# Reordering the second batch's attention and moving one cast in a fused attention and gated-MLP kernel

## The chip, the cores and the metric

The kernel runs on one core of one Trainium2 chip. The metric is the device time of one execution in microseconds. Three executions of the kernel before took 326.76, 326.96 and 328.4 us; the median is 326.96.

A core has five instruction streams that run side by side and wait for one another through semaphores: TensorE (PE, matrix products, with a separate row PEld for its weight loads), VectorE (DVE), ScalarE (ACT), GpSimd (POOL) and SyncE (SP, which here only issues DMA transfers). Each stream executes its own instructions in the order in which they were written. Sixteen DMA engines move data. Matrix products are accumulated in PSUM, a small memory that the other engines read from; everything else on the core lives in SBUF.

## The reference

```python
def _attn_ref(q, k, v, g_norm):            # 8 batches, 8 heads, 576 positions, 64 columns
    kv = np.einsum('bhsd,bhse->bhde', k, v)
    out = np.einsum('bhsd,bhde->bhse', q, kv)
    rms = np.sqrt(np.mean(out * out, axis=-1, keepdims=True) + 1e-06)
    return (out / rms * g_norm)

def _moe_ref(x, w_gate, w_val, w_out, rms_g):   # 4608 tokens, 512 columns, 1536 inner columns
    rms = np.sqrt(np.mean(x * x, axis=-1, keepdims=True) + 1e-06)
    xn = x / rms * rms_g
    g = xn @ w_gate
    return (g * (1 / (1 + np.exp(-g))) * (xn @ w_val)) @ w_out
```

The attention has no softmax: each head forms a 64x64 matrix `kv` and multiplies q by it. Its output is normalised per head, laid out as 4608 rows of 512, and goes through a gated MLP that normalises each row again.

## The kernel before

**Tiling.** A batch has 576 positions: four chunks of 128 (`NC = 4`) and a remainder of 64. The heads are handled in pairs, four pairs (`NS = 4`). The MLP handles 512 positions at a time: group g is batch g without its remainder, and a last group, the ninth, takes the eight remainders, which are collected in `xr`. So the MLP of group g needs the attention of batch g, and while PE works on group g the attention of batch g + 1 is fitted between its matmuls.

**The MLP of a group** (L630 to L704). For each of 12 blocks of inner columns there is a gate slot (four matmuls into a PSUM tile of the pool `mm1`, then silu on ScalarE, L643) and a value slot (four matmuls, L634, then the product with the silu on VectorE, L652). Then 16 slots of three L669 matmuls multiply by `w_out`; the result is copied out of PSUM (L685) and stored by a DMA that SP issues. The first group (batch 0) is done differently, since its inputs come late: its 512 positions go in two halves of 256, so the gate and value matmuls are half as wide (12 pairs per half), and its second product runs over all four output tiles at once (`slots_b_by_j`, L728). Two of these four output tiles are in the pool `o2` and two in `mm1`, which has three buffers; the third was left over in these slots.

**Slots and order.** The second half of group 0 is 12 slots of one gate and value pair each (slots 0 to 11), then 16 slots of three L669 matmuls (12 to 27); group 1 begins with slot 28, which is `starts[1]`. A `Placer` holds a list of operations for each slot. `P.at(engine, cost, function, slot)` puts an operation into a given slot; `P.put` searches the first slot from a given one that has room for it on its engine, by costs and room that are written in tables (L21 to L28), and `P.psum` does it for PE work that needs one of the three `att` buffers in PSUM. `emit` (L746) then walks through the slots: first the other engines' operations of a slot, then the slot's own MLP matmuls, then its attention work on PE. This is the order in which every engine executes.

**The attention of batch 1** (`place_second`, L577, called with s = 9). All its places are written out by hand, as offsets from s. The steps:

- `qT_heads` (L304): transposes of q on PE, copied out by VectorE and ScalarE (L320).
- `kv_mm` (L260): 40 matmuls of 64 columns that form `kv` of all heads in one `att` buffer, and `kv_half` (L290), two copies of it on VectorE to SBUF (`kvs`).
- `oT_mm` (L363): the attention output transposed, one PSUM tile for each head pair (and one for the remainder); `sqT_` (L374) squares it on ScalarE into `sqT`.
- `o_mm` (L328): the attention output itself, one PSUM tile for each chunk; `outa_` (L359) copies it to SBUF as bf16 on VectorE, which frees its `att` buffer.
- `stat_mm` (L399): 20 small matmuls of `sqT` with the selection matrix `sel` (L407), which sum the squares per head, plain and weighted by the squared gain. With `guard=True` one more matmul (L402, in fp32, two passes in the profile) first writes `D * eps` into the plain sums, so that they are never zero.
- `lead_chain` (L428): from these sums the factor `al` for each row and head: a reciprocal, a product, a sum, one more operation on VectorE, a square root on ScalarE (its table is loaded ahead by `preload_act_table`, L608, and silu's after it, L441), and a reciprocal.
- `xna_` (L479): output times factor, one instruction for each chunk, on VectorE.
- `xT_mm` (L502) and `xT_out` (L515): transposes on PE for the MLP, two chunks and two head pairs at a time, copied out with the gain by ScalarE (pairs `P0`) and VectorE (pairs `P1`).

In `place_second` oT and o of a part come in turn, o is copied, and the guard is PE's.

**The attention of batches 2 to 7** (`place_attention`, L553) is placed by searching. It takes its squares from o, multiplies them by the squared gain on POOL (L414), and computes the factor on VectorE. q is transposed by DMA on SP (L324, L326) once it has been cast to bf16; k and v are loaded and cast by DMAs that POOL issues (L185: 512 KB and a remainder of 64 KB each); x is transposed by DMA on SP (L540). The cast of q comes from `place_casts` (L542): for batch 2 on ScalarE at three given slots, the first being `starts[1] - 9`, and it returns the slot from which q's transposes count as done; for later batches on POOL. Batch 3's k and v loads and its casts of q are put on POOL's list from group 1's slots 14 and 18 on.

## Time and profile before

| what | value |
|---|---|
| executions | 326.76, 326.96, 328.4 us |
| the profiled execution: time, and span from its first to its last instruction | 326.35 us, 324.6 us |
| mean granted clock of TensorE | 0.999 |
| PE busy, 37 to 62 us | 24.72 of 25.00 us |
| PE busy, 62 to 94 us | 32.00 of 32.00 us |
| DMA traffic, 37 to 62 us and 62 to 94 us | 203 and 158 GB/s |
| SP's transposes of batch 2's q, issued | 57.19 and 58.72 us |
| SP's transposes of batch 2's x, issued | 86.13 and 88.08 us |

The page gives, for one execution, the busy time of each engine and the chain of work that ended last, followed back from the end. A line of a timeline gives the start in us, the duration, the engine, the line of the kernel, the operation, output <- input with shapes, how many instructions were merged into the line, and in brackets the idle time before and what ended it. PE's matmuls overlap: a matmul of 512 columns is shown with 0.38 us, and the next starts 0.216 us after it. ScalarE and VectorE instructions overlap by about 0.1 us in the same manner. DMA rows give the size of a transfer and the time from its issue to its landing.

Group 0's second half ends at 44.81 us, its second product at 59.68 us; group 1 ends at about 93.8 us.

### The profile page before, as it was taken

To read this page: it belongs to the slowest core of one execution; us is meant where nothing else is said; L and a number is where in the kernel's file an instruction comes from. 1 tells how busy PE (TensorE), PEld (TensorE's weight loads), DVE (VectorE), ACT (ScalarE), POOL (GpSimd) and SP (SyncE) were. 2 spreads that over 40 slices of the span, in tenths; PEclk is the share of its full clock that TensorE was granted. 3 is DMA by queue.
4 is the path that set the end of the run, shared out by engine and by line. 5 is a ranking of instruction groups with operands and counts; after the bars stand their busy time and mean duration, and the time that the engine had idled before them with its cause. 6 is when DMAs were issued, how large, how long until landed. Compare 5 with 4: busy or idle time off the path is not lost.

```text
span 324.6 us, 5420 instructions
## 1 busy us (share of the span) xinstructions
PE 316.2 (97%) x2060; PEld 162.2 (50%) x2060; DVE 177.0 (55%) x392; ACT 144.5 (45%) x269; POOL 89.4 (28%) x109
## 2 busy tenths in 40 slices
PE   7889999999999999999999999999999999999995
PEld 2478865554454445444544445444544444444443
DVE  3458457679938671858186818681778133203411
ACT  1375546686658323832284227422742233223320
POOL 8753330039106700670058005800420000000000
PEclk9999999999999999999999999999999999999999
DMA  8999999965994995499558956796100800020013
GB/s 194 228 200 200 191 220 221 203 161 72 163 210 124 127 162 142 140 118 149 147 158 101 139 149 178 87 138 165 35 1 0 172 32 0 29 102 0 0 34 97
DMA packets 78741, 40.49 MB, mean 125 GB/s; under 512 B 42744, under 2 KB 74236, under 8 KB 78716
## 3 DMA queue, kind: packets, MB, share of 16 engines
q0 software_dynamic: 30928, 14.16, 34.4%
q1 hardware_dynamic: 46048, 25.08, 32.6%
q10 hardware_dynamic: 1740, 0.92, 1.0%
q8 instruction: 16, 0.26, 0.3%
q14 instruction: 9, 0.07, 0.1%
HBM read 37.78 MB, written 9.44 MB: 145 GB/s over the span
## 4 chain that ended last, share of the span: by engine, by line
PE 95%; DMA 3%; DVE 1%; issue 0%; POOL 0%; ACT 0%; DVEq 0%; POOLq 0%
PE mm L634 57%; PE o L669 26%; DMA vc<-in_v_dram 3%; PE att L331 2%; PE att L268 2%; PE mm L669 2%; PE o L698 1%; PE att L509 1%; PE o L368 0%; PE mm L279 0%; PE att L368 0%; PE mm L662 0%; PE att L309 0%; PE mm L232 0%; PE att L340 0%
## 5 line engine op out<-in xcount | busy, mean ns | idle before, releaser
L652 DVE TENSOR_TENSOR h<-silu,mm 128x512 bf16<-128x512 bf16 (+1 forms) x120 | 75.7, 632 | 84.5 <-PE mm L634 78.7
L643 ACT ACTIVATE silu<-mm 128x512 bf16<-128x512 f32 (+1 forms) x120 | 66.3, 555 | 83.0 <-PE mm L634 73.7
L634 PE MATMUL mm<-x,wv 128*128 128x512 bf16 (+1 forms) x432 | 99.8, 355 | 0.0
L634 PE MATMUL mm<-x,wg 128*128 128x512 bf16 (+1 forms) x420 | 98.7, 358 | 0.0
L669 PE MATMUL o<-wo,h 128*128 128x512 bf16 x396 | 89.9, 379 | 0.0
L414 POOL TENSOR_TENSOR sq<-sq,g 128x512 bf16<-128x512 bf16 x30 | 34.7, 1156 | 130.9 <-ACT sq L357 130.9
L634 PEld LDWEIGHTS <-wv 128*128 128x128 bf16 x480 | 46.2, 98 | 44.0
L634 PEld LDWEIGHTS <-wg 128*128 128x128 bf16 x468 | 44.6, 98 | 42.4
L669 PEld LDWEIGHTS <-h 128*128 128x128 bf16 x420 | 40.3, 98 | 46.9
L685 ACT COPY osb<-o 128x512 f32<-128x512 f32 x33 | 19.2, 587 | 69.5 <-PE o L669 69.5
L419 DVE TENSOR_REDUCE st<-sq 128x8 f32<-128x512 bf16 x60 | 38.9, 678 | 1.2 <-ACT sq L357 0.8
L292 DVE CAST kvs<-att 64x256 bf16<-64x256 f32 x14 | 5.9, 422 | 29.9 <-PE att L268 29.7
L483 DVE TENSOR_TENSOR xna<-outa,al 128x512 bf16<-128x512 bf16 x35 | 21.8, 684 | 0.0
L357 ACT ACTIVATE sq<-att 128x512 bf16<-128x512 f32 x30 | 17.9, 596 | 2.2 <-PE att L331 2.2
L361 ACT CAST outa<-att 128x512 bf16<-128x512 f32 x30 | 17.7, 589 | 0.0
L331 PEld LDWEIGHTS <-qTs 128*128 128x128 bf16 x140 | 10.3, 98 | 6.6
L331 PE MATMUL att<-kvs,qTs 128*128 128x128 bf16 x140 | 12.7, 219 | 0.0
L634 PE MATMUL mm<-xr,wg 128*128 128x512 bf16 x48 | 12.3, 379 | 0.0
L634 PE MATMUL mm<-xr,wv 128*128 128x512 bf16 x48 | 12.3, 379 | 0.0
L203 POOL CAST main_q<-stg 128x1024 bf16<-128x1024 f32 (+1 forms) x12 | 11.4, 997 | 0.1
L232 PE MATMUL mm<-idle 128*128 128x512 bf16 x27 | 8.4, 471 | 2.1 <-DVE idle L161 2.1
L786 ACT ACTIVATE wv<-wv,gain 128x384 bf16<-128x384 bf16 x16 | 9.1, 609 | 0.0
(130 smaller groups left out, 172.3 us busy)
## 6 DMA issues: line engine op xcount, KB each, us to landing
out_dram<-osb SPq DMA_DIRECT2D x32, 256.0 KB, 2.4
stg<-in_q_dram SPq DMA_DIRECT2D x6, 1024.0 KB, 6.5
vc<-in_v_dram POOLq DMA_DIRECT2D x7, 512.0 KB, 8.4
kc<-in_k_dram POOLq DMA_DIRECT2D x7, 512.0 KB, 6.1
wg<-in_moe_w_gate_dram POOLq DMA_DIRECT2D x4, 384.0 KB, 15.8
wv<-in_moe_w_val_dram POOLq DMA_DIRECT2D x4, 384.0 KB, 16.9
wo<-in_moe_w_out_dram POOLq DMA_DIRECT2D x4, 384.0 KB, 13.8
stg<-in_k_dram SPq DMA_DIRECT2D x2, 512.0 KB, 6.7
```

The source lines that it names most:

```text
L203: return copy(out=mains[b, t][:, cs[0] : cs[1], h0:h1, :], in_=staged[b, t].rearrange("p h (c d) -> p c h d", c=NC)[:, cs[0] : cs[1], h0:h ...
L331: nc.tensor.matmul(o[:, 2 * j : 2 * j + 2, :], lhsT=self.qTj[:, j, c, :], rhs=self.kv[:, j, :, :], start=j == 0, stop=j == NS - 1, skip_gr ...
L357: nc.scalar.activation(out=self.sq[c][:, 0], in_=self.o[c], func=ACT.Square)
L361: (eng.tensor_copy if eng else nc.scalar.copy)(out=self.outa[c], in_=self.o[c])
L414: eng.tensor_tensor(out=self.sq[c][:, 1], in0=self.sq[c][:, 0], in1=g2, op=OP.mult)
L419: nc.vector.reduce_sum(out=self.st[:, which, c, :], in_=self.sq[c][:, which], axis=AX.X)
L483: return eng.tensor_tensor(out=self.xna[:, c], in0=src, in1=self.al[:, c, :].to_broadcast([128, H, D]), op=OP.mult)
L634: nc.tensor.matmul(ps[:, : c1 - c0], lhsT=w[n][:, s, jj * 128 : (jj + 1) * 128], rhs=x_of(g, s, c0, c1), start=s == 0, stop=s == NS - 1)
L643: nc.scalar.activation(out=sis[g, j][:, c0:c1], in_=ps, func=ACT.Silu)
L652: nc.vector.tensor_tensor(out=hs[g, j][:, c0:c1], in0=sis[g, j][:, c0:c1], in1=v_ps, op=OP.mult)
L669: nc.tensor.matmul(ps, lhsT=hs[g, j][:, t * 128 : (t + 1) * 128], rhs=wo[j // OB][:, j % OB, :], start=j == 0, stop=j == NF - 1)
L685: (eng.copy if eng is nc.scalar else eng.tensor_copy)(out=o, in_=ps)
```

## The change

For batch 1, `kv_mm` moves from slot s + 2 to s, and its copies from s + 3 to s + 1. All five oT steps come first, then the statistics (at s + 6 in place of s + 8), then the five o steps. o is no longer copied to SBUF: `xna_` reads it from PSUM, which holds each o tile until its product; the third of them uses the free buffer of `mm1`. The guard is added by VectorE in `lead_chain`, with one `tensor_scalar`, and not by a matmul. The products and the final transposes come three slots sooner, with the two transposes of a pair one slot apart. The floor for the next batch's PE work goes from slot s + 20 to s + 18. For batch 2, the three operations that cast q on ScalarE move from slots 19 to 21 to slots 24 to 26, and the slot from which q's transposes count as done from 30 to 32. The tables and all other batches' code are the same; what is placed by searching may come out at other slots. Behind the edit the line numbers are three lower (L634 becomes L631).

```diff
-        def stat_mm(self, c0, c1, guard=False):
+        def stat_mm(self, c0, c1):
             self.st = st = att_p.tile([128, 2, NC + 1, H], FP32, name="att")
-            if guard:
-                nc.tensor.matmul(
-                    st[:, 0, c0:c1, :], lhsT=ones, rhs=epsr[:, : (c1 - c0) * H], start=True, stop=True, skip_group_check=True,
-                )
...
-                        start=not guard and c == c0 and j == 0, stop=c == c1 - 1 and j == NS - 1,
+                        start=c == c0 and j == 0, stop=c == c1 - 1 and j == NS - 1,
...
-        def lead_chain(self, c0, c1):
+        def lead_chain(self, c0, c1, guard=False):
...
             u = self.st[:, 0, cs]
+            if guard:
+                u = self.u[:, cs]
+                V.tensor_scalar(out=u, in0=self.st[:, 0, cs], scalar1=D * eps, scalar2=None, op0=OP.add)
             V.reciprocal(out=r, in_=u)
...
-            return [op, ("DMA", at + 11)]
+            return [op, ("DMA", at + 8)]
...
-        P.at("PE", 1.14, lambda: a.kv_mm(range(NS)), s + 2)
-        dve(3, 0.43, lambda: a.kv_half(0))
-        dve(3, 0.43, lambda: a.kv_half(1))
+        P.at("PE", 1.14, lambda: a.kv_mm(range(NS)), s)
+        dve(1, 0.43, lambda: a.kv_half(0))
+        dve(1, 0.43, lambda: a.kv_half(1))
 
         parts = [((j,), 0, NC) for j in range(NS)] + [(ALL, NC, NC + 1)]
-        oT = lambda n: pe((3, 4, 4, 5, 6)[n], 0.25, ("oT", n), lambda: a.oT_mm(*parts[n]))
-        o = lambda n: P.at("PE", 0.24, lambda: a.o_mm(n), s + (3, 4, 5, 5, 6)[n])
-        for f, n in ((oT, 0), (o, 0), (oT, 1), (o, 1), (oT, 2), (o, 2), (oT, 3), (o, 3), (oT, 4), (o, 4)):
-            f(n)
         for n in range(NC + 1):
-            act((4, 5, 5, 6, 7)[n], 0.62, lambda n=n: a.sqT_(ps["oT", n], *parts[n]))
-            dve((4, 5, 6, 6, 7)[n], 0.69, lambda n=n: a.outa_(n, V))
-        P.at("PE", 0.64, lambda: a.stat_mm(0, NC + 1, True), s + 8)
-        act(8, 1.28, lambda: A.preload_act_table(ACT.Sqrt))
-        dve(9, 2.0, lambda: a.lead_chain(0, NC + 1))
+            pe((2, 2, 3, 4, 5)[n], 0.25, ("oT", n), lambda n=n: a.oT_mm(*parts[n]))
+            act((3, 4, 4, 5, 6)[n], 0.62, lambda n=n: a.sqT_(ps["oT", n], *parts[n]))
+        act(6, 1.28, lambda: A.preload_act_table(ACT.Sqrt))
+        P.at("PE", 0.64, lambda: a.stat_mm(0, NC + 1), s + 6)
+        for n in range(NC + 1):
+            P.at("PE", 0.24, lambda n=n: a.o_mm(n, mm1_p if n == 2 else None), s + (7, 7, 8, 9, 10)[n])
+        dve(7, 2.2, lambda: a.lead_chain(0, NC + 1, True))
         for c in range(NC + 1):
-            dve(10 + c, 0.68, lambda c=c: a.xna_(c, V))
-        for at, cs in ((15, (0, 1)), (17, (2, 3))):
-            for js, eng in ((P0, "ACT"), (P1, "DVE")):
-                P.at("PE", 0.24, lambda js=js, cs=cs: a.xT_mm(js, cs), s + at)
+            dve(9 + c, 0.68, lambda c=c: a.xna_(c, V, a.o[c]))
+        for at, cs in ((12, (0, 1)), (14, (2, 3))):
+            for n, (js, eng) in enumerate(((P0, "ACT"), (P1, "DVE"))):
+                P.at("PE", 0.24, lambda js=js, cs=cs: a.xT_mm(js, cs), s + at + n)
                 for j in js:
-                    P.at(eng, 0.4, lambda j=j, cs=cs, e=engs[eng]: a.xT_out(j, cs, e), s + at + 1)
-        P.at("PE", 0.15, lambda: a.xT_mm(ALL, (NC,)), s + 19)
-        dve(20, 0.62, lambda: [a.xT_out(j, (NC,), V) for j in ALL])
-        P.floor = s + 20
+                    P.at(eng, 0.4, lambda j=j, cs=cs, e=engs[eng]: a.xT_out(j, cs, e), s + at + n + 1)
+        P.at("PE", 0.15, lambda: a.xT_mm(ALL, (NC,)), s + 16)
+        dve(17, 0.62, lambda: [a.xT_out(j, (NC,), V) for j in ALL])
+        P.floor = s + 18
...
-            casts = place_casts(P, 2, starts[1] - 9)
+            casts = place_casts(P, 2, starts[1] - 4)
```

## The prediction

> **What bounds the kernel now.** I read the page first, the busy rows and the chain.

> ```profile
> span 324.6 us, 5420 instructions
> PE 316.2 (97%) x2060; PEld 162.2 (50%) x2060; DVE 177.0 (55%) x392; ACT 144.5 (45%) x269; POOL 89.4 (28%) x109
> PE   7889999999999999999999999999999999999995
> PE 95%; DMA 3%; DVE 1%; issue 0%; POOL 0%; ACT 0%; DVEq 0%; POOLq 0%
> ```

> TensorE works nearly all the time and is 95% of the chain that ended last. So a change is worth only the gaps it takes out of PE or puts in. By stretch, PE is busy 24.72 of 25 us from 37 to 62 and 32.00 of 32 from 62 to 94. The edit lies in the first stretch; nothing there can give more than its gaps and the PE work it drops. Second, PE in order of time around the second batch's attention:

> ```profile
> 44.00 0.88 PE L268 MATMUL att<-vc,kc 128*64 128x64 bf16 x40
> 45.26 0.38 PE L669 MATMUL mm<-wo,h 128*128 128x512 bf16 x1
> 45.91 0.39 PE L368 MATMUL att<-qTs,kvs 128*128 128x512 bf16 x1 [0.28 <-DVE kvs L292]
> 51.45 0.41 PE L402 MATMUL att<-epsr,ones 1*128 1x40 f32 x2
> 51.80 0.65 PE L407 MATMUL att<-sel,sqT 128*128 128x4 bf16 x20
> 59.68 1.03 PE L634 MATMUL mm<-x,wg 128*128 128x512 bf16 x4
> ```

> A wait of 0.28 for the kv copies, the guard (0.34 in the chain), and batch 1's first gate at 59.68. Third, where the next edge is: POOL's list and the landings of batch 3's k and v, and what PE does with them (columns of the loads: size, us from issue to landing).

> ```profile
> 75.51 0.94 POOL L192 DMA_DIRECT2D kc<-in_k_dram  x1
> 76.46 1.16 POOL L414 TENSOR_TENSOR sq<-sq,g 128x512 bf16<-128x512 bf16 x1
> 77.56 2.02 POOL L203 CAST main_q<-stg 128x1024 bf16<-128x1024 f32 x2
> 79.53 0.60 POOL L210 CAST remq<-rstg 64x512 bf16<-64x512 f32 x1
> 80.09 0.75 POOL L188 DMA_DIRECT2D kc<-in_k_dram  x1
> 81.70 0.70 POOL L188 DMA_DIRECT2D vc<-in_v_dram  x1
> ```

> ```profile
> kc<-in_k_dram POOLq DMA_DIRECT2D x1, 512.0 KB, 6.0
> vc<-in_v_dram POOLq DMA_DIRECT2D x1, 512.0 KB, 8.4
> kc<-in_k_dram POOLq DMA_DIRECT2D x1, 64.0 KB, 4.4
> vc<-in_v_dram POOLq DMA_DIRECT2D x1, 64.0 KB, 9.4
> x<-xna SPq DMA_TRANSPOSE x2, 5.5
> ```

> ```profile
> 92.35 0.88 PE L268 MATMUL att<-vc,kc 128*64 128x64 bf16 x40
> 93.16 0.82 PE L669 MATMUL o<-wo,h 128*128 128x512 bf16 x3
> 93.82 1.03 PE L634 MATMUL mm<-x,wg 128*128 128x512 bf16 x4
> ```

> The last v load lands at 81.70 + 9.4 = 91.1, kv needs it at 92.35. The second transpose of batch 2's x is issued at 88.08 and taken alone lands 5.3 later, at 93.4; the gate at 93.82 needs it. Only 1.2 and 0.4 us are spare there.

> **The change, part by part.**

> *kv sooner.* PE runs 12 groups of half width from 38.66 to 43.9, 0.437 each. kv moves ahead of the last four, to 42.16. Its copies (0.86 on VectorE) hide behind four groups, 1.75: the 0.28 goes. Without that cover it would be back. The second 64 KB of k was issued at 26.97 and landed 13.8 later, 40.8, so 1.4 us are spare.

> *Guard.* Two matmuls, 0.34, leave PE. VectorE gets one addition on 128x40, 0.21 (L455), 0.25 with its gap.

> *oT first, o in PSUM.* PE's operations stay the same. From the end of the half groups, 44.81, PE needs 48 L669 at 0.216 = 10.37, five oT 1.08, statistics 0.59, five o 1.10, four xT groups 0.90. The statistics follow twelve L669 and five oT: 44.81 + 2.59 + 1.08 = 48.48, done 49.1. From the reciprocal to the first product took 1.84 (52.49 to 54.33); with the addition 2.09, so products run from 51.4, one each 0.60. A product from PSUM takes 682 ns (L350, 128x512), from SBUF 684 (L483): no price, and five copies of 690 leave VectorE, which is not on the path. Held buffers: the fifth o needs the first product (52.1) and comes at 44.81 + 24 L669 + 1.08 + 0.59 + 0.88 = 52.5, 0.4 spare, the smallest margin; the first xT comes at 54.1 and needs the second product at 52.7. The square-root table (1.28) follows the fifth square, some 48.5 to 49.8, and is wanted at 50.6. So nothing here stops PE. If the chain ran over 0.4 late, the fifth o and all of PE would pay the rest.

> *The cast later.* ScalarE now does the last x pair first. PE gives it at 44.81 + 36 L669 + 1.08 + 0.59 + 1.10 + 0.45 = 55.8, finished 56.2; pair 0.84, casts 1.99, remainder 0.5, then the copy of the output in the mm buffer, 0.58: 60.1. Queued behind it are two output copies and the first silu. PE's gate starts at 44.81 + 14.16 = 58.97 (the small transposes, 0.12, are now before it), so it compares with 59.68 + 0.12: 0.83 sooner. The first value matmul wants that mm buffer at 59.83: it waits 0.3 for ScalarE. Bounds 0 and 0.6 (one output copy more or less). Net **-0.55**. The cast's end moves from 57.2 to 59.0, and the transposes of q it releases on SP too, with four output stores and the next q load queued behind them; q was landed by about 61.3 (windows of the queue's traffic) and is used at 65.9 before, some 67 after, so this is hidden by 4 us.

> *What the two steps move on POOL.* In the built program's order batch 2's attention is later by one or two groups of 0.86, and POOL's list changes: the 512 KB of k for batch 3 now stands behind the fifth product, both casts and the remainder. The fifth square stays near 76, so POOL issues k at 76.4 + 1.1 + 2.0 + 0.5 = 80.0 instead of 75.5, the other three loads about 0.85 later. Before, this k crossed in DMA time that nobody else used (77.3 to 81); now it meets q's transposes (the 64 KB of k, issued 80.09, needed 4.4 to land behind them), v, and x's transposes on SP from 86.1. Its cost: in batch 4, loads back to back, v lands at 107.26 + 8.2 = 115.46 and the 64 KB before it at 106.58 + 5.7 = 112.28: 3.2 for 512 KB.

> The last v then lands between 90.3 (batch 4's 10.28 from first issue to last landing, from 80.0) and 91.1 + 3.2 = 94.3; kv wants it at 91.8. The x transpose lands between 93.4, unmoved, and 96.6; the gate wants it at 93.27. From 89.5 to 90.8 the DMA engines moved 11 GB/s, so 1.2 us of that stretch can take up work. I take 3.2 - 1.2 = 2.0 for x: landing 95.4, gate at 95.45 against 93.82, **+1.6** in place of -0.55. Who goes first decides which of the two is late: from 111 to 114 the software queue (k, v) had 1389 packets and SP's queue none, though q's transpose was issued at 110.91. That says v first and x late. From 50 to 52 both queues had 336 packets each.

> [...]

> *Sum.* PE has no gap from there on and the instruction order after it is as before, so +1.6 reaches the end: the profiled execution (324.6 span, 326.35 with what lies around it) becomes 327.95. The median of the runs shown is 326.96, 0.61 above it; the same +1.6 there gives **328.6**.

> **Rivals.**

> *Not slower:* the DMA engines take k in among the rest, v lands at 90.3 to 91.1 and x at 93.4. For it: batch 4's loads take 10.28 altogether, and over 62 to 94 the traffic is only 158 GB/s. Against: from 83 to 89 it is dense already. It decides if k costs under 0.4 us of x's landing: gate at 93.27 to 93.45, -0.55 to -0.4, 326.5.

> [...]

> *No slack found:* x pays the whole 3.2 and lands at 96.6: +2.8, 329.8.

> *k of batch 1 late:* kv at 42.16 stands on a landing at 40.8; 64 KB loads in the crowded stretch took 13.8 to 17.8 us, so up to 2.6 of wait, less 0.55: 329.0.

> *The held PSUM stops PE*, so that the edit doesn't do what it says: the fifth o waits. Each 0.4 beyond the margin costs as much; 327.5.

> **Chances.** Forecast 0.35, not slower 0.25, v late 0.20, no slack 0.10, k late 0.05, held PSUM 0.05. A measurement of this kernel can tell about 0.5% from no change, 1.63 us, 328.6: the forecast stands on that line, so half of it counts as slower. With most of the second, third and fourth rivals: slower 0.50, same 0.45. Faster by as much would need gaps that PE doesn't have (at most 0.83): 0.05. The range goes from the first rival to somewhat past the third, 326.3 to 330.3; the forecast's own is 327.9 to 329.3.

> **What would show it.** PE: no wait before the first oT, no L402, gate near 59.0, value matmul waiting some 0.3 for an output copy. POOL: k's issue near 80. Then a PE wait of 1 to 3 us near 92 to 95, before kv (DMA v) or the gate (DMA x). If PE is gapless there the forecast is wrong and the time is 326.5; if the largest gap lies between 42 and 62, I have mis-sized the part that was edited.

## The result, and the profile after

The changed kernel takes **332.57 us** (median of 4 executions, 331.63 to 333.39), the kernel before in the same series 326.86 (326.61 to 328.4). The ratio is **1.0171, 95% interval 1.0155 to 1.0188**: slower by 5.7 us, where 1.6 were forecast and the range ended 2.3 us lower. The profiled execution took 332.66 us with a span of 330.9, 6.3 more than the 324.6 before.

Rows of the changed kernel's page (the span, busy times, PE's busy tenths and its granted clock in 40 slices, the chain by engine):

```profile
span 330.9 us, 5392 instructions
PE 316.1 (96%) x2037; PEld 163.2 (49%) x2058; DVE 173.7 (53%) x388; ACT 144.6 (44%) x269; POOL 89.1 (27%) x109
PE   7789999999949999999999999999999999999995
PEclk9999999999968999999999999999999999999999
PE 87%; DMA 7%; POOL 2%; issue 1%; ACT 1%; DVE 0%; POOLq 0%
```

PE's busy time is the same, and one slice of 40, the twelfth (91 to 99 us), has fallen to 4 tenths. The chain has 7% of DMA where it had 3. The clock row shows a second loss: TensorE ran that slice and the next at less than its full clock. Neither slice lies where the kernel was edited.

PE's timeline around the edit (start and duration in us):

```profile
42.80 0.88 PE L268 MATMUL att<-vc,kc 128*64 128x64 bf16 x40
45.58 0.38 PE L368 MATMUL att<-qTs,kvs 128*128 128x512 bf16 x1
59.44 1.03 PE L631 MATMUL mm<-x,wg 128*128 128x512 bf16 x4
60.47 1.02 PE L631 MATMUL mm<-x,wv 128*128 128x512 bf16 x4
```

After kv and the half-width matmuls behind it, the first oT (L368) starts without a wait. From the first gate matmul to the first value matmul are 1.03 us, some 0.17 more than the 0.86 between the next ones: that is the wait for ScalarE's late copy. The first gate starts 0.24 sooner than before, although this execution's start phase ran later: PE's first transpose of q (L309) is at 37.96 us, before at 37.42 (batch 0's kv, whose code is the same, waited 1.8 us for v, before 1.2). The marks for a comparison without the start phase are that transpose, the first output matmul of group 1 (L666, before L669) and batch 3's first o (L331); first the kernel before, then the changed one:

```profile
37.42 1.31 PE L309 MATMUL att<-ident,qc 128*64 128x128 bf16 x40
82.55 9.88 PE L669 MATMUL o<-wo,h 128*128 128x512 bf16 x45
95.54 0.61 PE L331 MATMUL att<-kvs,qTs 128*128 128x128 bf16 x8
```

```profile
37.96 1.31 PE L309 MATMUL att<-ident,qc 128*64 128x128 bf16 x40
82.35 9.88 PE L666 MATMUL o<-wo,h 128*128 128x512 bf16 x44
```

From the first mark to the second it took 82.55 - 37.42 = 45.13 us before and 82.35 - 37.96 = 44.39 now. So the edited stretch **gives 0.74 us**.

PE's timeline of the changed kernel where group 1 ends:

```profile
95.44 0.40 PE L268 MATMUL att<-vc,kc 128*64 128x64 bf16 x4 [3.22 <-DMA vc<-in_v_dram]
96.65 1.28 PE L268 MATMUL att<-vc,kc 128*64 128x64 bf16 x36 [0.81 <-DMA vc<-in_v_dram]
98.26 1.06 PE L666 MATMUL o<-wo,h 128*128 128x512 bf16 x2 [0.33 <-issue]
99.11 1.91 PE L631 MATMUL mm<-x,wg 128*128 128x512 bf16 x4
101.83 0.61 PE L331 MATMUL att<-kvs,qTs 128*128 128x128 bf16 x8
```

Batch 3's kv stands 3.22 us for v and its second part 0.81 more. Then the work itself is slow: 36 matmuls of kv take 1.28 us where all 40 took 0.88, four gate matmuls 1.91 instead of 1.03. Before, kv came 9.80 us after the group's first output matmul, so here it was due at 82.35 + 9.80 = 92.15. Batch 3's first o (L331) starts at 101.83, 9.68 later; before it was 3.19 (92.35 to 95.54). Of the 6.49 lost, 4.03 are the two waits and the rest, some 2.5, is mostly the slow work around them. With 0.74 gained and the start phase 0.54 later the sum is 6.3, the difference of the spans.

The clock in windows of 3.41 us in the changed kernel, one core (columns: window and its length, then busy us and instructions of PE, PEld, DVE, ACT and POOL, granted clock, DMA share, GB/s):

```profile
90.88:94.29 3.41, 1.35 (x7) 0.39 (x4) 0.00 (x0) 0.03 (x1) 0.00 (x0) 1.00 1.55 155
94.29:97.70 3.41, 1.45 (x40) 1.40 (x40) 0.00 (x0) 0.00 (x0) 0.00 (x0) 0.50 1.34 185
97.70:101.11 3.41, 3.08 (x13) 1.28 (x11) 1.39 (x4) 1.15 (x3) 0.00 (x0) 0.50 0.38 121
101.11:104.52 3.41, 3.41 (x26) 1.92 (x25) 1.78 (x5) 3.22 (x7) 1.15 (x1) 1.00 0.90 268
```

In the first window PE worked 1.35 of 3.41 us; for the next two the clock was granted at half, although PE was busy for 3.08 us of the third. In these two windows PE worked 1.45 + 3.08 = 4.53 us at half clock. If all of that work takes twice as long, half of it, some 2.3 us, is the loss; this is an estimate, and it fits the 2.5 above. The mean granted clock of the other executions points the same way: 0.989 at 332.48 and 333.39 us, and 0.993, about one window less of half clock, at 331.63, the fastest.

Why v was late, POOL's timeline and the landings (size, median us from issue to landing) in the changed kernel:

```profile
77.53 2.02 POOL L203 CAST main_q<-stg 128x1024 bf16<-128x1024 f32 x2
79.49 0.61 POOL L210 CAST remq<-rstg 64x512 bf16<-64x512 f32 x1
80.05 0.94 POOL L192 DMA_DIRECT2D kc<-in_k_dram  x1
82.55 0.71 POOL L188 DMA_DIRECT2D vc<-in_v_dram  x1
```

```profile
kc<-in_k_dram POOLq DMA_DIRECT2D x1, 512.0 KB, 8.7
vc<-in_v_dram POOLq DMA_DIRECT2D x1, 512.0 KB, 13.6
kc<-in_k_dram POOLq DMA_DIRECT2D x1, 64.0 KB, 8.7
vc<-in_v_dram POOLq DMA_DIRECT2D x1, 64.0 KB, 14.1
x<-xna SPq DMA_TRANSPOSE x2, 9.8
```

The 512 KB of k is issued at 80.05 instead of 75.51, behind both casts of q. Every row is then slower than it was: the last v 14.1 instead of 9.4 (landing at 82.55 + 14.1 = 96.6 instead of 91.1), x's two transposes 9.8 instead of 5.5. Both queues suffer.

### The profile page after: what moved, and what is told of

It reads as the page before. It is cut to its first block, busy times and chain, and to the rows that moved or that the text cites. A ratio compares the mean times of both kernels' runs of the same rounds, so it can differ in the third digit from the quotient of the medians.

```text
span 330.9 us, 5392 instructions
## 1 busy us (share of the span) xinstructions
PE 316.1 (96%) x2037; PEld 163.2 (49%) x2058; DVE 173.7 (53%) x388; ACT 144.6 (44%) x269; POOL 89.1 (27%) x109
## 3 DMA queue, kind: packets, MB, share of 16 engines
q0 software_dynamic: 30928, 14.16, 34.0%
## 4 chain that ended last, share of the span: by engine, by line
PE 87%; DMA 7%; POOL 2%; issue 1%; ACT 1%; DVE 0%; POOLq 0%
PE mm L631 54%; PE o L666 23%; DMA vc<-in_v_dram 7%; PE att L331 2%; PE att L268 2%; PE mm L666 1%; POOL main_q L203 1%; PE o L695 1%; PE att L508 1%; PE o L368 0%; POOL sq L410 0%; PE mm L279 0%; PE mm L659 0%; PE att L309 0%; PE mm L232 0%
## 5 line engine op out<-in xcount | busy, mean ns | idle before, releaser
L631 PE MATMUL mm<-x,wv 128*128 128x512 bf16 (+1 forms) x431 | 99.7, 356 | 0.0
L631 PE MATMUL mm<-x,wg 128*128 128x512 bf16 (+1 forms) x419 | 99.5, 360 | 0.1
L666 PE MATMUL o<-wo,h 128*128 128x512 bf16 x383 | 88.0, 380 | 1.5 <-issue 1.0
L631 PEld LDWEIGHTS <-wv 128*128 128x128 bf16 x480 | 46.4, 98 | 44.5 <-issue 1.1
L631 PEld LDWEIGHTS <-wg 128*128 128x128 bf16 x468 | 44.9, 98 | 43.1 <-issue 1.1
L666 PEld LDWEIGHTS <-h 128*128 128x128 bf16 x420 | 40.3, 98 | 46.1 <-issue 0.3
L292 DVE CAST kvs<-att 64x256 bf16<-64x256 f32 x14 | 5.9, 422 | 34.6 <-PE att L268 34.5
L482 DVE TENSOR_TENSOR xna<-outa,al 128x512 bf16<-128x512 bf16 x30 | 18.7, 682 | 0.0
L331 PEld LDWEIGHTS <-qTs 128*128 128x128 bf16 x140 | 10.2, 98 | 6.8
L631 PE MATMUL mm<-xr,wg 128*128 128x512 bf16 x47 | 12.3, 379 | 0.1
L631 PE MATMUL mm<-xr,wv 128*128 128x512 bf16 x47 | 12.3, 379 | 0.1
L331 PE MATMUL att<-kvs,qTs 128*128 128x128 bf16 x136 | 12.2, 219 | 0.0
L203 POOL CAST main_q<-stg 128x1024 bf16<-128x1024 f32 (+1 forms) x12 | 11.4, 997 | 0.1
L268 PE MATMUL att<-vc,kc 128*64 128x64 bf16 x280 | 6.9, 203 | 4.0 <-DMA vc<-in_v_dram 4.0
## 6 DMA issues: line engine op xcount, KB each, us to landing
vc<-in_v_dram POOLq DMA_DIRECT2D x7, 512.0 KB, 8.5
kc<-in_k_dram POOLq DMA_DIRECT2D x7, 512.0 KB, 6.4
wo<-in_moe_w_out_dram POOLq DMA_DIRECT2D x4, 384.0 KB, 14.1
stg<-in_k_dram SPq DMA_DIRECT2D x2, 512.0 KB, 7.2
```

Of the source, the lines that this page charges most:

```text
L203: return copy(out=mains[b, t][:, cs[0] : cs[1], h0:h1, :], in_=staged[b, t].rearrange("p h (c d) -> p c h d", c=NC)[:, cs[0] : cs[1], h0:h ...
L331: nc.tensor.matmul(o[:, 2 * j : 2 * j + 2, :], lhsT=self.qTj[:, j, c, :], rhs=self.kv[:, j, :, :], start=j == 0, stop=j == NS - 1, skip_gr ...
L482: return eng.tensor_tensor(out=self.xna[:, c], in0=src, in1=self.al[:, c, :].to_broadcast([128, H, D]), op=OP.mult)
L631: nc.tensor.matmul(ps[:, : c1 - c0], lhsT=w[n][:, s, jj * 128 : (jj + 1) * 128], rhs=x_of(g, s, c0, c1), start=s == 0, stop=s == NS - 1)
L666: nc.tensor.matmul(ps, lhsT=hs[g, j][:, t * 128 : (t + 1) * 128], rhs=wo[j // OB][:, j % OB, :], start=j == 0, stop=j == NF - 1)
```

## The experiments

Each kernel is the changed one with one edit, unless it says "before". Times are medians; ratios are to the kernel before, run beside it on the same chip.

**1. k ahead of the fifth product again.** Only the place of one DMA issue on POOL's list is put back.

```diff
-            for f in loads_kv(b + 1):
-                P.put("POOL", 0.85, f, at=starts[b - 1] + 14)
+            for n, f in enumerate(loads_kv(b + 1)):
+                if b == 2 and n == 0:
+                    P.at("POOL", 0.85, f, starts[1] + 15)
+                else:
+                    P.put("POOL", 0.85, f, at=starts[b - 1] + 14)
```

> The changed kernel with one instruction moved: batch 3's 512 KB load of k stands on POOL ahead of the fifth product again, as in the kernel before. Theory 1 (the loss is this load's place: v lands late behind it, PE waits 4.0 us and runs 2.1 us at a lower clock): no wait at batch 3's kv, last v landed by 91.5, TensorE's granted clock 1.00 from 92 to 103, and the time is that of the kernel before less what the edit in batch 1 gives, 0.6 to 0.8: 326.0 to 326.4. Theory 2 (the loss comes from batch 2's attention or x's transposes being later, the load is a bystander): a wait of 2 us or more near 92 to 95 stays, 329 or more.

Measured: **326.09 us, ratio 0.9985 (0.9975 to 0.9994)**, span 324.5. POOL's timeline, the landings, and PE's timeline of this kernel:

```profile
75.75 0.94 POOL L192 DMA_DIRECT2D kc<-in_k_dram  x1
76.71 1.17 POOL L410 TENSOR_TENSOR sq<-sq,g 128x512 bf16<-128x512 bf16 x1
```

```profile
kc<-in_k_dram POOLq DMA_DIRECT2D x1, 512.0 KB, 6.2
...
vc<-in_v_dram POOLq DMA_DIRECT2D x1, 64.0 KB, 8.8
x<-xna SPq DMA_TRANSPOSE x2, 4.9
```

```profile
92.32 0.88 PE L268 MATMUL att<-vc,kc 128*64 128x64 bf16 x40
93.36 0.59 PE L666 MATMUL o<-wo,h 128*128 128x512 bf16 x2 [0.16 <-issue]
93.79 1.03 PE L631 MATMUL mm<-x,wg 128*128 128x512 bf16 x4
```

With k issued at 75.75 all landings are short again, kv does not wait, the clock stays at 1.00, and the whole loss is gone. The place of this one transfer is the cause; what else the change does costs less than it gives (0.47 us less than the 326.56 of before on this chip).

**2. The same loads late, in the kernel before.** The reverse: without the change in batch 1, all four loads of batch 3 stand behind the casts of q.

```diff
+            for n, f in enumerate(loads_kv(b + 1)):
+                if b == 2:
+                    P.at("POOL", 0.85, f, starts[1] + 23)
+                else:
+                    P.put("POOL", 0.85, f, at=starts[b - 1] + 14)
```

> The kernel before with one thing of the changed kernel: all four loads of batch 3's k and v stand on POOL behind its cast of q. Theory 1: the same loss without any of the edit: last v lands some 14 us after its issue, near 96, kv waits some 4 us, the clock falls to 0.5, 332 to 333.5. Theory 2: k and v land in time or wait under 1 us, 326.5 to 328.

Measured: **330.0 us, ratio 1.0099 (1.0084 to 1.0115)**, span 328.0. PE's timeline:

```profile
94.28 0.28 PE L268 MATMUL att<-vc,kc 128*64 128x64 bf16 x4 [1.44 <-DMA vc<-in_v_dram]
95.41 0.82 PE L268 MATMUL att<-vc,kc 128*64 128x64 bf16 x36 [0.84 <-DMA vc<-in_v_dram]
97.26 1.02 PE L634 MATMUL mm<-x,wg 128*128 128x512 bf16 x4 [0.28 <-DMA x<-xna]
```

The late loads alone make the kernel before slower: direction as expected, size too large in the expectation. v landed at 82.69 + 12.7 = 95.4 and kv was due at 92.84, so the waits sum to 2.3 instead of 4.0, and the clock stayed at 1.00 (36 matmuls in 0.82). That is the profiled execution, of 329.83 us. The mean granted clock of all four shows that it was not always so: 0.997 and 1.000 at 329.83 and 329.23 us, 0.994 and 0.993 at 330.18 and 330.40. The kernel before, whose clock falls in the profile only after its last matmul (at 323.75 us), has 0.997 to 1.000 in all executions run beside the experiments, and a half clock for 3.41 us takes 0.5 x 3.41 / 328 = 0.005 from the mean. So in two of the four the clock most likely fell once, for 3.41 us. The waits and the fall of the clock are two things, and the second does not follow from every wait.

**3. PE kept busy while it waits.** 14 idle matmuls of 512 columns ahead of batch 3's kv; nothing uses their result.

```diff
+            if self.b == 3:
+                spin(mm1_p.tile([128, MAIN], FP32, name="mm1"), 14)
```

> The changed kernel with 14 idle matmuls of 512 columns (3.0 us) ahead of batch 3's kv, which fill most of PE's wait and add work that the result doesn't use. Theory 1 with the clock as a cost of its own: v lands as before, but PE is not idle for 3 us, so the clock stays at 1.00 and the 2.1 us of slow work behind the wait go: 330.2 to 330.8. Rival (the clock falls for another reason, or the slow work is a matter of contention): 332 to 333.

Measured: **330.01 us, ratio 1.0104 (1.0087 to 1.0121)**, span 327.4, clock 1.00 in every window from 80 to 104 us. v is still late (kv starts at 94.89), but its 40 matmuls then take 1.16, and the gate starts at 96.63. The useless work makes the kernel faster by 332.57 - 330.01 = **2.6 us**, or 2.3 when each is first compared with before in its own series (5.7 and 3.45 us slower). As the cost of the halved clock this is an upper bound: in the profiled execution v's 64 KB landed 12.9 us after their issue, 1.2 less than in the changed kernel's, so a part of it may be an earlier v.

**4. Five idle matmuls in place of 14**, the same edit with 5.

> The kernel after, with 5 instead of 14 idle matmuls of 512 columns ahead of batch 3's kv on TensorE (their result is used by nothing). They take about 5 x 0.22 = 1.1 us once the accumulator is free, so that TensorE still stands for about 2.1 us of the 3.2 it stood, and then 0.8 between the two parts of kv. Data bound alone: the end of the wait stays where v lands, 95.4 to 96.7 us, in this run as in the one with 14. Theory, the clock falls for the length of one stop: a stop of 2.1 us is nearer to the 1.44 and 0.84 that left it at 1.00 than to the 3.2 that halved it, so 1.00 throughout from 92 to 104 and a time of 330.0 +- 0.4 us, as with 14. Rival, the clock answers to the share of time TensorE stood in the stretch, not to one unbroken stop: 2.1 and 0.8 us out of 4 would still lower it, a slice at 0.5 and a time of 331.5 to 332.6.

Measured: **330.65 us (329.46 to 331.26), ratio 1.012 (1.0091 to 1.015)**. PE's timeline of the profiled execution:

```profile
91.83 1.24 PE L232 MATMUL mm<-idle 128*128 128x512 bf16 x5
95.04 0.28 PE L270 MATMUL att<-vc,kc 128*64 128x64 bf16 x4 [1.97 <-DMA vc<-in_v_dram]
96.25 0.82 PE L270 MATMUL att<-vc,kc 128*64 128x64 bf16 x36 [0.93 <-DMA vc<-in_v_dram]
97.67 1.03 PE L633 MATMUL mm<-x,wg 128*128 128x512 bf16 x4
```

Waits of 1.97 and 0.93 left the clock at 1.00 in this execution, and the last v landed 13.9 us after its issue, almost as in the changed kernel. So these two can be set side by side: from kv's second part to batch 3's first o it is 101.83 - 96.65 = 5.18 us there and 99.39 - 96.25 = 3.14 here, and the halved clock cost **2.0 us**. The four times spread by 1.8 us, more than with 14, and the mean granted clock goes with them: 1.000 and 0.998 at 330.21 and 329.46 us, 0.995 and 0.993 at 331.10 and 331.26. So in two executions out of four the clock most likely fell once, as in experiment 2, and these were about 1.3 us slower. The expectation's theory, that a stop of this length leaves the clock at 1.00, therefore holds in the profiled execution and fails in two others. The length of a stop that is safe stays open.

**5. x behind v.** SP's first transpose of batch 2's x, and so all that is queued behind it on SP, waits for batch 3's last v load.

```diff
...
+            if self.b == 2 and c0 == 0:
+                tc.add_manual_dep(t.ins, made[3, 2].ins.name, SYNC, reason="v first")
...
```

> The changed kernel, where SP's first transpose of batch 2's x (and all that SP issues behind it) waits for the landing of batch 3's last v load. If x's transposes stretched the loads (the two queues share the DMA engines), the last v lands 10 to 11 us after k's issue, at 90.3 to 91.3 instead of 96.6, kv doesn't wait or waits under 0.3, and the wait moves to the gate behind x, which lands 4 to 5 us after v, at 95 to 96: a wait of 1.5 to 2.5 us there, 328 to 329.5. If the loads were slow by themselves, the last v still lands at 95 or later and x later yet: 335 or more.

Measured: **332.7 us, ratio 1.0184 (1.0169 to 1.02)**, a clear miss. v still landed late, at 82.39 + 11.6 = 94.0, and now x was late as well. PE's timeline:

```profile
93.70 1.16 PE L270 MATMUL att<-vc,kc 128*64 128x64 bf16 x40 [1.63 <-DMA vc<-in_v_dram]
98.77 1.49 PE L636 MATMUL mm<-x,wg 128*128 128x512 bf16 x4 [3.16 <-DMA x<-xna]
```

So x's transposes are not all that v collides with.

**6. q's transposes and all behind them after v** (a single execution). SP's transposes of batch 3's q, which precede the output store and x on SP's list, wait for the last v load.

```diff
...
+            if self.b == 3:
+                tc.add_manual_dep(t.ins, made[3, 2].ins.name, SYNC, reason="v first")
...
-        load = P.put("SP", 0.0, a.qT_dma, casts[:1] if b == 2 else casts)
+        load = P.put("SP", 0.0, (lambda: None) if b == 3 else a.qT_dma, casts[:1] if b == 2 else casts)
+        if b == 3:
+            P.at("SP", 0.0, a.qT_dma, starts[1] + 25)
```

> The changed kernel, where SP's transpose of batch 3's q, and with it all that SP issues behind it (batch 2's first output store and x), waits for the landing of batch 3's last v load. With x alone held back the last v landed 14.1 us after the start of k's issue; batch 4's needed 10.3. If q's transposes and the store in front of k make up the rest, k lands 6.0 to 6.5 after its issue and the last v 10.2 to 11 after it, near 90.5, and kv doesn't wait; x is later still and the gate waits 3 us or more, 331 to 335. If the last v again lands 13 or more after k's issue, something other than SP's queue slows the loads.

Measured: 333.51 us, span 331.7. The landings of this kernel, and PE's timeline:

```profile
kc<-in_k_dram POOLq DMA_DIRECT2D x1, 512.0 KB, 6.1
...
vc<-in_v_dram POOLq DMA_DIRECT2D x1, 64.0 KB, 8.3
x<-xna SPq DMA_TRANSPOSE x2, 3.4
```

```profile
91.71 0.88 PE L270 MATMUL att<-vc,kc 128*64 128x64 bf16 x40
99.67 1.89 PE L640 MATMUL mm<-x,wg 128*128 128x512 bf16 x4 [6.33 <-DMA x<-xna]
```

With SP's queue silent the last v lands at 82.10 + 8.3 = 90.4, though k was issued as late as 79.60, and kv does not wait. Now x pays, 6.33 us. From k's issue to the last v landing it took 16.6 us in the changed kernel (80.05 to 96.6), 14.1 with x held back, 10.8 with q's transposes held back too. By these three traces the transfers of SP add 5.8 us to v: 2.5 come from x's transposes and what follows them, 3.3 from q's transposes and the output store. Each figure is one execution, and where SP's queue was left as it is, the same stretch took 15.2 (experiment 2), 15.4 (3) and 16.4 us (4). So the whole is 4.4 to 5.8, and the part of x the less certain of the two. A late k is harmless to v in itself; it is late into a stretch that SP's transfers fill.

**7. The number that moved it.** The change also altered the slot from which q's transposes count as done, 30 to 32. Here it is 30, and all else is as in the changed kernel.

```diff
-            return [op, ("DMA", at + 8)]
+            return [op, ("DMA", at + 6)]
```

> The changed kernel with one number changed: place_casts returns slot 30, not 32, from which batch 2's q counts as transposed; the casts themselves stay late. In the built program batch 2's attention then starts two groups sooner and the searching puts batch 3's 512 KB of k ahead of the fifth product, by itself. Theory 1 (the whole loss is the two slots that push this load behind the cast): 326.0 to 326.4, no wait from 90 to 100, batch 2's first product from q's transposes not late. Rival (the later cast itself costs: q's transposes land too late for two slots less): a PE wait before batch 2's first o near 66 of 0.5 us or more, 327 or more.

Measured: **325.86 us, ratio 0.9974 (0.9963 to 0.9984)**, 326.63 for before on this chip. Faster than both kernels. POOL issues k at 75.19 again, batch 2's first o (at 66.43) does not wait for q, and PE's timeline shows kv and the gate without a wait:

```profile
92.03 0.88 PE L268 MATMUL att<-vc,kc 128*64 128x64 bf16 x40
92.84 0.82 PE L666 MATMUL o<-wo,h 128*128 128x512 bf16 x3
93.50 1.03 PE L631 MATMUL mm<-x,wg 128*128 128x512 bf16 x4
```

**8 and 9. All four loads early, in the changed kernel and in the kernel before.** They stand at slot 8 of group 1 in both, so the two kernels differ in the edit alone and not in the loads' place.

```diff
...
+                if b == 2:
+                    P.at("POOL", 0.85, f, starts[1] + 8)
...
```

> The changed kernel with all four loads of batch 3's k and v put on POOL's list from slot 8 of group 1, some 15 us before its cast of q, into DMA time that is little used. Theory 1: the same as with the one load restored, since nothing behind is waited for: 325.9 to 326.4; all four landed by 82. Rival (POOL's 3.3 us of issuing and the traffic hold up batch 2's products, its statistics and x): x lands past 93.3 and the time is 327 or more.

> The kernel before with the same early loads. If its margins of 1.2 us (v) and 0.4 us (x) were enough, it gains nothing: 326.4 to 326.9, and the difference to the changed kernel with early loads, 0.5 to 0.8, is what the edit in batch 1 is worth. If it gains 0.5 or more, the kernel before already lost time to late landings in runs without a profile.

Measured: changed 326.14 us (0.9984, 0.9974 to 0.9993), before 326.93 (1.0011, 1.0001 to 1.002). Before gains nothing from early loads: they were early enough; it is even 0.3 us slower with them. The difference, **0.79 us, is what the edit is worth** with the loads at one place, close to the 0.74 of the trace. Against the kernel before as it stands it is less, 326.63 - 326.14 = 0.49, and 0.47 in experiment 1, so 0.5 to 0.8 is as much as the runs show.

## Why the prediction was wrong

- *What bounds, and where the edit can give:* right. What changed is a gap at one place, and the clock behind it.
- *kv sooner, guard, oT first, o in PSUM:* right. No wait before the first oT, none for held PSUM, kv at 42.80 without waiting for k. From the guard's addition to the first product it takes 51.86 - 49.72 = 2.14 us, forecast 2.09; the addition is 0.20 of it. The rivals "k of batch 1 late" and "held PSUM" fell.
- *The cast later:* the mechanism right, the term too large: the value matmul waits about 0.17, not 0.3. These 0.13 are most of the step from -0.55 to the measured -0.74.
- *POOL's order:* right to the place: k issued at 80.05, forecast 80.0. Experiment 7 adds which number did it: the two slots by which batch 2's attention was placed later.
- *The landing of v, at most 94.3:* **this step failed first.** The price of k, 3.2 us, was taken from batch 4, whose loads cross back to back, and added to before's landing as if the other queue's transfers kept their times. It landed at 96.6, so k's later place cost 5.5 us and not 3.2; experiment 6 shows 4.4 to 5.8 us of v's time to be the sharing with SP's transfers. x was mis-sized by the same step: its second transpose was issued at 88.11 and landed 9.4 later, at 97.5, against a bound of 96.6.
- *Who goes first:* wrong. I let x decide and v go ahead, on a stretch of the kernel before (111 to 114 us) in which only the software queue had packets, 1389 to none. Here both move: from 90 to 94 us the software queue had 845 packets and SP's 791; from 86 to 90, in which x's transposes were issued (86.32 and 88.11), 1476 against 312. An even share, as from 50 to 52 in the kernel before (336 each), is what the first of these stretches shows and the second does not; no run shows what sets the shares. "v late", given 0.20, is what came, but larger: at its bound of 94.3, v is 2.5 us behind the 91.8 at which kv wanted it, and waits of 4.0 were found.
- *The sum:* **its missing term was the clock.** The sum, and every rival, turned a wait into time one for one. The clock's row, and experiments 3 and 4, show that the waits of 3.22 and 0.81 us cost about 2 to 2.6 us beyond themselves, because TensorE's granted clock fell to half for 6.82 us.
- "Not slower" failed because the engines had no idle time to take k in: the 1.2 us that I found from 89.5 to 90.8 was gone, since x and v were still crossing (1789 packets from 86 to 90 us, 1637 in the next four).

So the 5.7 us are the edit's -0.74 (forecast -0.55), waits of 4.0 (forecast 2.2, from -0.55 to +1.6) and a clock loss of 2.0 to 2.6 (forecast nothing). With the measured waits and gain but without the clock the sum would have been 326.96 - 0.74 + 4.03 = 330.2, just inside the range; the clock carried the time out of it.

## What to carry to other kernels

When an edit delays a transfer, do not add the duration that it has alone (here 3.2 us for k, where v came 5.5 later): look at what the other queues move in its new place, and stretch all of them. A wait of a few microseconds on TensorE may have to be priced with the work behind it at half clock (here at 3.2 us, and in some executions of experiments 2 and 4, whose profiled waits were 1.4 and 2.0 us), so see whether a few idle matmuls (14 gave back 2.3 to 2.6 us in experiment 3), or better an earlier issue (the whole loss in experiment 1), keep it short. When a scheduler places operations by search, compare the order on every queue after the change, and put one transfer back before judging the edit: here one number separated 1.7% slower from 0.26% faster.

## What the runs showed of the hardware

The clock returned after windows with 3.08 (the changed kernel), 3.41 (experiment 5) and 2.64 us (experiment 6) of work; the changed kernel's window with 1.45 was followed by another at half.

**SP's transfers and the casting loads of k and v slowed each other.** The 64 KB of v took 8.3 us to land with SP's queue held back and 14.1 with it active, x's transposes 3.4 (issued after v had landed) and 9.8. Which of the two gave way differed by stretch (1476 packets of the software queue to 312 of SP's from 86 to 90 us, 845 to 791 from 90 to 94), and no run here isolates what sets it.
